# Splitting the expert weights into halves on ScalarE and VectorE instead of GpSimd, with the float32 blocks moved one place and a new order of issue

## The chip, the cores and the metric

One core of one Trainium2 chip. The metric is the device time of one execution in microseconds (us), median of the runs. The work is clustered attention for 4 batches of 768 tokens with 8 heads of 64, followed by a feed-forward layer (512 to 2048 to 512) on the 3072 tokens.

## The reference

```python
def _attn_ref(q, k, v, centroids):
    ...
    q_assign = np.argmax(np.einsum('bhsd,hcd->bhsc', q_n, c_n), axis=-1)
    k_assign = np.argmax(np.einsum('bhsd,hcd->bhsc', k_n, c_n), axis=-1)
    mask = q_assign[:, :, :, None] == k_assign[:, :, None, :]
    scores = scale * np.matmul(q, k.transpose(0, 1, 3, 2))
    scores = np.where(mask, scores, -1000000000.0)
    ...
    return np.matmul(attn, v).astype(np.float32)

def _moe_ref(x, w_in, w_out):
    h = x @ w_in
    ...
    g = np.where(pos, h, np.where(neg, 0.0, (h + beta) ** 2 / (4.0 * beta)))
    return (g @ w_out).astype(np.float32)
```

`q_n`, `k_n`, `c_n` are the rows divided by their norms, `attn` is the softmax over the keys, `pos` and `neg` are `h >= 1` and `h <= -1`. `w_in` and `w_out` arrive as float64.

## The kernel before, in words

**Units.** The tokens of a batch are cut into three chunks of 256 queries; a chunk of a batch is a unit `u`, 12 in all. A unit has four head pairs `hp`, and a pair has four score tiles of 128 queries by 768 keys (`at_scores`): 192 tiles. TensorE writes a tile to PSUM (`pair`), VectorE adds the bias for the cluster mask, takes it to SBUF (`sS`, a ring of three buffers) and finds the row's bound `sbi` in one custom instruction, ScalarE takes the exponential (`at_soft`), casts it to float16 as `hl`'s first half, GpSimd subtracts to get the second half, and a DMA transposes both into `pT`. `at_av` multiplies by the values. For unit 0 transposes by TensorE stand in place of the DMA. From step 22 on the scores use `pair[0]` alone; `pair[1]` gathers the feed-forward layer's output.

**Precision.** Matmuls of float32 accuracy are made from float16 halves: a value is scaled by a power of two, `hi` is its cast, `lo` is the value minus `hi`, and three products of halves are summed. Unit 0 is the exception: its feed-forward layer multiplies in float32, straight from the weights' float32 blocks, since the halves are not there yet.

**Weights.** The feed-forward layer goes by 8 blocks `f` of 256 hidden columns; each has a block of `w_in` (`a = 0`) and one of `w_out` (`a = 1`), 16 blocks `i = 2f + a` of 128 x 1024 values. `w_load` brings one as float64, `w_bits` makes float32 of its bits (a shift and two bit operations on VectorE, an absolute value on ScalarE, sums on TensorE, their maximum `w_am`), `w_bound` makes the scales `w_sw` for four `f` at a time (`GF = 4`), and `w_split` makes the halves `w1[f]`, `w2[f]`.

All 16 blocks lie in one tensor `wb`, 1024 words a block. The float32 values of block `i` lie at place `i` (`w32`, line 1049), and so do the halves: 2 x 1024 float16 values fill the same 1024 words. So `w_split` first copies the scaled values out, to a buffer `tf`, and then writes over the block (line 1138):

```python
tf = wk[1].bitcast(F32) if f < EARLY_SPLITS else new("ws", [1024], F32)
...
rec.scalar.activation(out=tf, in_=w32[a][f].bitcast(F32), func=AF.Copy, scale=w_sw[:, f, a : a + 1])
rec.scalar.copy(whi, tf)
rec.gpsimd.tensor_tensor(out=wlo, in0=tf, in1=whi, op=ALU.subtract)
```

For the first four `f` (`EARLY_SPLITS`) `tf` is `wk[1]`, for the rest a ring of `wk[0]` and the two halves of `word`. These buffers serve other ends too: `wk[0]` is a scratch of `w_bits`, `wk[1]` takes half of the last raw block, `word` is a raw block's place, and all of them are among the seven buffers of the ring `x`, which holds the attention output of a unit for its feed-forward layer.

**What sets the order.** No instruction is issued where it is written. `rec` (class `Recorder`) notes each with its cost and what it depends on; `at(step, fn, ...)` gives each function a step; `issue` (line 328) turns the steps into priorities, runs a list scheduler forward and backward `BASE` times over a model of the engines, adds a number of small pseudo-random shifts to the priorities, one for each number in `NUDGES`, and issues in the order of the last forward pass. So every instruction's line in the profile is 342, and groups are told apart by their tiles. Each engine works its own list in order.

Of the kernel before, what the change touches and what calls it, by code (L numbers as in the profile page):

```python
# [11 lines left out]
F32 = mybir.dt.float32  # L12
U32 = mybir.dt.uint32
AF = mybir.ActivationFunctionType
# [26 lines left out]
TURN, TURN_WAIT = dict(vector=185, gpsimd=118), 200  # L41

LOOK, MARGIN = 0.4, 4000
BASE = 9
NUDGES = (
# [17 lines left out]
)  # L63
TILED = 248

# [400 lines left out]
def tile_clustered_attention_moe(  # L466
# [35 lines left out]
    EARLY = 22  # L502
    VL = 9
    VB = 4
    EARLY_SPLITS = 4
    WA, WR = -4, 2.6

    RAW = [3, 4, 5, 6, 7, 4, 5, 6, 0, 7, 6, 7, 0, 7, 0, None]
# [5 lines left out]
    def tiles(name, n, size):  # L514
        return [const.tile([P, size // 4], U32, name=f"{name}{i}") for i in range(n)]
# [17 lines left out]

    wk = tiles("wk", 2, 4096)
    word = tiles("word", 1, 8192)[0]
    rings["w32"], rings["x"] = Ring(wk[:1] + rings["o"].bufs), Ring(tiles("x", 3, 4096) + wk + [word[:, :1024], word[:, 1024:]])
    rings["g"] = Ring(tiles("g", 2, 2048))

    nb = tiles("n", 1, 2 * 3072)[0]
    nats = [nb[:, :768], nb[:, 768:]] + rings["x"].bufs[1:3]  # L540

    wb = tiles("w", 1, 2 * NF * 4096)[0]
    raws = [wb[:, n * 2048 : (n + 1) * 2048] for n in range(NF)]
# [72 lines left out]
    def v_bound(b, hp):  # L616

        if b == 0:
            st = view(slots[hp][:, 1536:2304], [2 * T * D], F32)
        else:  # L620
            st = view(rings["x"].bufs[2], [2 * T * D], F32) if b == 1 else new("vb", [2 * T * D], F32)
            rec.sync.dma_start(st.rearrange("p (h f) -> p h f", h=2), heads(v, b, hp))
        e = BX.setdefault(b, {})
        if hp == 0:
            e["am"] = new("v_am", [NP], BF16, 2)
        rec.vector.tensor_reduce(
            out=e["am"][:, hp : hp + 1], in_=st, op=ALU.max, axis=AX.X, apply_absolute_value=True
        )
# [417 lines left out]

    W = {}
    WL, WS = {}, {}
    w32 = [[wb[:, (2 * f + a) * 1024 : (2 * f + a + 1) * 1024] for f in range(NF)] for a in range(2)]
    w1 = [view(wb[:, 2 * f * 1024 : (2 * f + 1) * 1024], [2, DM // P, 256], F16) for f in range(NF)]  # L1050
    w2 = [view(wb[:, (2 * f + 1) * 1024 : (2 * f + 2) * 1024], [2, 2, DM], F16) for f in range(NF)]

# [3 lines left out]
    WP = {}  # L1056

    wd = 2 if w_wide else 1
    rings["ws"] = Ring([wk[0], word[:, :1024], word[:, 1024:]])

    def w_load(a, f, part=None):

# [73 lines left out]
        rec.vector.reciprocal(sw, iw)  # L1136

    def w_split(a, f):
        tf = wk[1].bitcast(F32) if f < EARLY_SPLITS else new("ws", [1024], F32)
        w = (w1 if a == 0 else w2)[f]  # L1140
        whi, wlo = (w[:, x].rearrange("p a f -> p (a f)") for x in range(2))
        rec.scalar.activation(out=tf, in_=w32[a][f].bitcast(F32), func=AF.Copy, scale=w_sw[:, f, a : a + 1])
        rec.scalar.copy(whi, tf)
        rec.gpsimd.tensor_tensor(out=wlo, in0=tf, in1=whi, op=ALU.subtract)


    F = {}
# [112 lines left out]
    for b in range(B):  # L1260
# [11 lines left out]
        for c in range(NCH):  # L1272
            u = b * NCH + c
            s0 = first(b, 0, c)
            for x, fn in zip((PRO, -9.1, -8.1, -6.1) if u == 0 else (s0 - 14, s0 - 6.8, s0 - 6.4, s0 - 4.5), (q_load, q_scale, q_split, q_assign)):
                at(x, fn, u)
            for hp in range(0, NP, NP if c else 1):
                at(first(b, hp, c) - (5.5 if u == 0 else 3), q_pairs, u, hp, NP if c else 1)
            for hp in range(NP):
                s0 = first(b, hp, c)  # L1280
                for n in range(SC):
                    at(s0 + n, at_scores, b, hp, c, n // CT, n % CT)
                    at(s0 + n + 1, at_soft, b, hp, c, n // CT, n % CT)
                at(s0 + LA - 0.5, at_av, b, hp, c)

            sf = max(sf, s0 + FA, wat[-1] + 3 if u else 0)
            if u == 1 or u and c == 0:
                at(sf - 1, ffn_scale, range(u, (b + 1) * NCH), range(NF))
            for f in range(NF):
                if u == 0:  # L1290
                    sf = max(sf, wat[2 * f + 1] + 2)
                    FS[u, f] = dict(io=1.0, first=f == 0, last=f == NF - 1)
                    for x in range(2):
                        at(max(sf + 3.5, (wat[-1] if f >= EARLY_SPLITS else wat[2 * GF - 1] if f < GF else wat[-1]) + 1), w_split, x, f)
                    if f == EARLY_SPLITS - 1:
                        free = max(sf + 3.5, wat[2 * GF - 1] + 1) + 0.1
                at(sf, ffn1, u, f)
                at(sf + 3, ffn2, u, f)
                sf += 2
    for i in range(2 * NF):  # L1300
        f, a = divmod(i, 2)
        last = max((k for k in range(i) if RAW[k] == RAW[i]), default=None)
        t0 = max(PRO + 2 + i, -1 if not RAW[i] else PRO) if last is None else wat[last | 1] + 0.1
        for p in (None,) if RAW[i] is not None else (0, 1):
            at(max(t0, free) if p is not None else t0, w_load, a, f, p)
            at(wat[i], w_bits, a, f, p)
        if a and f % GF == GF - 1:
            at(wat[i] + 0.5, w_bound, f // GF)
# [40 lines left out]
```

## Time and profile before

| | |
|---|---|
| median of 3 runs | 852.37 us (851.2 to 853.75) |
| profiled execution, its own time | 852.93 us |
| its span from first to last instruction | 851.1 us |
| PE (TensorE) busy | 810.1 us, 95% |
| DVE (VectorE) busy | 635.3 us, 75% |
| ACT (ScalarE) busy | 656.1 us, 77% |
| POOL (GpSimd) busy | 536.2 us, 63% |
| granted TensorE clock, mean | 0.993 |

The profiled execution lies 0.56 us above the median. The busy shares are means over the whole span; the stages differ, so the text reads them by stretch. PEld is the load of a matmul's weights, which runs beside other matmuls. SP issues the DMAs.

### The profile page before, as it was taken

To read this page: it belongs to the slowest core of one execution; us is meant where nothing else is said; L and a number is where in the kernel's file an instruction comes from. 1 tells how busy PE (TensorE), PEld (TensorE's weight loads), DVE (VectorE), ACT (ScalarE), POOL (GpSimd) and SP (SyncE) were. 2 spreads that over 40 slices of the span, in tenths; PEclk is the share of its full clock that TensorE was granted. 3 is DMA by queue.
4 is the path that set the end of the run, shared out by engine and by line. 5 is a ranking of instruction groups with operands and counts; after the bars stand their busy time and mean duration, and the time that the engine had idled before them with its cause. 6 is when DMAs were issued, how large, how long until landed. Compare 5 with 4: busy or idle time off the path is not lost.

```text
span 851.1 us, 18767 instructions
## 1 busy us (share of the span) xinstructions
PE 810.1 (95%) x7052; PEld 558.9 (66%) x7052; DVE 635.3 (75%) x1400; ACT 656.1 (77%) x1166; POOL 536.2 (63%) x510
## 2 busy tenths in 40 slices
PE   3787998999999999999999999999999999999998
PEld 3455675666775676766776667667766667676664
DVE  6999999879886877678888766678888766544322
ACT  7778989899987788688778788788778688776232
POOL 1112799879986678667666778656677667666122
PEclk9999999999999999999999999999999999999999
DMA  9968898798999879898998988999999887665100
GB/s 311 269 138 246 225 204 213 157 172 194 186 172 159 186 128 205 171 185 169 201 187 165 168 160 177 197 170 199 204 155 161 150 162 126 119 123 111 20 25 25
DMA packets 404763, 142.50 MB, mean 167 GB/s; under 512 B 372800, under 2 KB 396352, under 8 KB 404672
## 3 DMA queue, kind: packets, MB, share of 16 engines
q1 hardware_dynamic: 404672, 141.30, 82.1%
q8 instruction: 55, 0.90, 0.4%
q14 instruction: 36, 0.29, 0.1%
HBM read 40.40 MB, written 6.29 MB: 55 GB/s over the span
## 4 chain that ended last, share of the span: by engine, by line
PE 77%; DVE 12%; DMA 4%; issue 3%; ACT 2%; POOL 1%; SPq 0%; DVEq 0%; POOLq 0%; ACTq 0%
PE pair L342 39%; PE banka L342 10%; PE banki L342 9%; PE bankj L342 9%; PE bankh L342 9%; DVE sS L342 3%; DVE w L342 2%; DMA pT<-hl 1%; DVE bankh L342 1%; DMA q<-qn 1%; DMA kv<-n 1%; ACT sS L342 1%; DVE mx L342 1%; DMA kv<-x 1%; POOL hl L342 1%
## 5 line engine op out<-in xcount | busy, mean ns | idle before, releaser
L342 POOL TENSOR_TENSOR hl<-sS,hl 128x768 f16<-128x768 f32 x176 | 301.2, 1716 | 120.7 <-ACT hl L342 105.5
L342 PE MATMUL pair<-w,g 128*128 128x512 f16 (+1 forms) x1120 | 276.7, 392 | 0.7 <-DVE g L342 0.7
L342 ACT ACTIVATE sS<-sS,sbi 128x768 f32<-128x768 f32 x192 | 179.2, 933 | 73.9 <-DVE sbi L342 70.5
L342 DVE CUSTOM_DVE_ANT_0 sS<-pair,zero,er 128x768 f32<-128x768 f32 x192 | 194.3, 1012 | 53.6 <-PE pair L342 32.9
L342 PEld LDWEIGHTS <-w 128*128 128x128 f16 x2112 | 204.9, 98 | 42.7 <-issue 4.5
L342 PEld LDWEIGHTS <-g 128*128 128x128 f16 x1056 | 101.1, 98 | 107.2 <-issue 2.0
L342 PE MATMUL pair<-kv,q 128*128 128x384 f16 x768 | 158.1, 329 | 11.1 <-ACT pT L342 5.0
L342 ACT CAST hl<-sS 128x768 f16<-128x768 f32 x176 | 144.4, 825 | 9.3 <-DMA pT<-hl 7.9
L342 POOL TENSOR_TENSOR g<-r,g 128x512 f16<-128x512 f32 x80 | 96.4, 1205 | 56.4 <-ACT g L342 50.6
L342 PEld LDWEIGHTS <-q 128*128 128x128 f16 x992 | 78.9, 98 | 66.6 <-issue 22.8
L342 PE MATMUL banka<-pT,kv 128*64 128x256 f16 (+1 forms) x1680 | 105.7, 279 | 0.3 <-DMA pT<-hl 0.3
L342 PEld LDWEIGHTS <-kv 128*64 128x64 f16 (+1 forms) x1824 | 92.3, 108 | 5.0 <-DMA kv<-x 1.7
L342 ACT ACTIVATE r<-r,f_ra,f_rs 128x512 f32<-128x512 f32 x80 | 64.8, 810 | 35.0 <-DVE r L342 34.3
L342 PE MATMUL bankj<-x,w 128*128 128x256 f16 (+1 forms) x424 | 59.1, 292 | 0.6 <-DVE g L342 0.4
L342 ACT CAST g<-r 128x512 f16<-128x512 f32 x80 | 48.8, 611 | 11.8 <-DVE r L342 5.9
L342 POOL TENSOR_TENSOR qn<-qn,phi 128x256 f16<-128x256 f16 x48 | 31.9, 684 | 30.3 <-DVE phi L342 19.9
L342 PE MATMUL bankh<-x,w 128*128 128x256 f16 (+1 forms) x376 | 46.7, 277 | 0.6 <-DVE zs L342 0.5
L342 PE MATMUL banki<-x,w 128*128 128x256 f16 (+1 forms) x288 | 40.3, 291 | 0.9 <-DVE r L342 0.9
L342 PE MATMUL banki<-wk,w 128*128 128x256 f16 x312 | 37.0, 273 | 0.0
L342 ACT ACTIVATION_READ_ACCUMULATOR sS<-sS,sbi 128x1 f32 x192 | 36.1, 188 | 0.0
L342 ACT ACTIVATE q<-q,phi 128x512 f16<-128x512 f16 x48 | 33.0, 711 | 2.8 <-DVE phi L342 0.8
L342 DVE TENSOR_SCALAR r<-banki,f_lo,f_hi 128x512 f32<-128x512 f32 x27 | 21.8, 806 | 16.0 <-PE banki L342 10.0
(262 smaller groups left out, 1099.8 us busy)
## 6 DMA issues: line engine op xcount, KB each, us to landing
w<-in_moe_w_out_dram SPq DMA_DIRECT2D x14, 512.0 KB, 4.8
q<-in_q_dram SPq DMA_DIRECT2D x12, 512.0 KB, 5.4
kv<-in_k_dram SPq DMA_DIRECT2D x16, 384.0 KB, 4.0
kv<-in_v_dram SPq DMA_DIRECT2D x16, 384.0 KB, 4.4
out_dram<-o SPq DMA_DIRECT2D x11, 512.0 KB, 3.6
w<-in_moe_w_in_dram SPq DMA_DIRECT2D x10, 512.0 KB, 6.1
word<-in_moe_w_in_dram SPq DMA_DIRECT2D x6, 512.0 KB, 4.3
o<-in_v_dram SPq DMA_DIRECT2D x8, 384.0 KB, 3.9
```

What stands on the lines that cost most here:

```text
L342: fn(*args, **kw)
```

## The change

`w_split` loses its buffer and its GpSimd instruction. ScalarE writes the scaled cast straight to `whi`; VectorE computes value times scale minus `whi` in one instruction into `wlo` (the helper `split`, which `k_split`, `q_split` and `v_split` use). Both read the float32 block, so it must not lie where its own halves go: block `i` now lies at place `i + 1`, and the last in `xs[2]`, the third `x` buffer, which goes to the end of the ring `x`. The ring `ws`, `EARLY_SPLITS` and `free` go; the splits of a group of four `f` may now come as soon as that group's scales are there. `BASE` is 13, and `NUDGES` is another list.

```diff
-BASE = 9
+BASE = 13
 NUDGES = (
-    2100000010, 2100000020, 2100000029, 2100000041, 2100000053, 2100000117, 2100000135, 2100000137,
...
+    2050000002, 2050000003, 2050000007, 2050000022, 2050000023, 2050000032, 2050000033, 2050000038,
...
-    EARLY_SPLITS = 4
...
-    rings["w32"], rings["x"] = Ring(wk[:1] + rings["o"].bufs), Ring(tiles("x", 3, 4096) + wk + [word[:, :1024], word[:, 1024:]])
+    xs = tiles("x", 3, 4096)
+    rings["w32"], rings["x"] = Ring(wk[:1] + rings["o"].bufs), Ring(xs[:2] + wk + [word[:, :1024], word[:, 1024:], xs[2]])
...
-    w32 = [[wb[:, (2 * f + a) * 1024 : (2 * f + a + 1) * 1024] for f in range(NF)] for a in range(2)]
+    w32 = [wb[:, i * 1024 : (i + 1) * 1024] for i in range(1, 2 * NF)] + [xs[2]]
+    w32 = [w32[a::2] for a in range(2)]
...
-    rings["ws"] = Ring([wk[0], word[:, :1024], word[:, 1024:]])
...
     def w_split(a, f):
-        tf = wk[1].bitcast(F32) if f < EARLY_SPLITS else new("ws", [1024], F32)
+        tf, sw = w32[a][f].bitcast(F32), w_sw[:, f, a : a + 1]
         w = (w1 if a == 0 else w2)[f]
         whi, wlo = (w[:, x].rearrange("p a f -> p (a f)") for x in range(2))
-        rec.scalar.activation(out=tf, in_=w32[a][f].bitcast(F32), func=AF.Copy, scale=w_sw[:, f, a : a + 1])
-        rec.scalar.copy(whi, tf)
-        rec.gpsimd.tensor_tensor(out=wlo, in0=tf, in1=whi, op=ALU.subtract)
+        split(whi, wlo, tf, sw)
...
-                        at(max(sf + 3.5, (wat[-1] if f >= EARLY_SPLITS else wat[2 * GF - 1] if f < GF else wat[-1]) + 1), w_split, x, f)
-                    if f == EARLY_SPLITS - 1:
-                        free = max(sf + 3.5, wat[2 * GF - 1] + 1) + 0.1
+                        at(max(sf + 3.5, wat[2 * GF * (f // GF + 1) - 1] + 1), w_split, x, f)
...
-            at(max(t0, free) if p is not None else t0, w_load, a, f, p)
+            at(t0, w_load, a, f, p)
```

The list itself tells nothing; what it does stands in the order that each engine gets. Three places follow. Names carry the number of their buffer; `ISA sS...<-pair...` is the custom instruction that takes a score tile, `v_am` the bound of a head pair's values, `w_78` the tensor `wb`.

VectorE, up to the first score tile, before:

```order
L342 TENSOR_TENSOR er_139<-bankj,zm_143 128x4
L342 TENSOR_REDUCE v_am_155<-kv_61 128x1
L342 TENSOR_REDUCE w_am<-banki 128x2
L342 SCALAR_TENSOR_TENSOR banki<-ik_130,iq_126 128x1
L342 ISA sS_86,sbi_144<-pair_79,zero,er_139 128x768
```

and now (the reduction of `kv_61` stands further ahead, between the query halves and the first key half):

```order
L342 TENSOR_TENSOR er_139<-bankj,zm_143 128x4
L342 SCALAR_TENSOR_TENSOR banki<-ik_130,iq_126 128x1
L342 TENSOR_REDUCE v_am_155<-kv_62 128x1
L342 TENSOR_SCALAR banki<-banki 128x1
L342 TENSOR_REDUCE v_am_155<-kv_63 128x1
L342 TENSOR_REDUCE v_am_155<-kv_64 128x1
L342 RECIPROCAL phi_142<-banki 128x1
L342 ISA sS_86,sbi_144<-pair_79,zero,er_139 128x768
```

All four reductions of batch 0 now stand ahead of the first score tile, where one did.

GpSimd, in the second unit of batch 0, while the float32 feed-forward layer of unit 0 runs, before:

```order
L342 TENSOR_TENSOR rr_159<-rs_149,rr_159 128x4
L342 TENSOR_TENSOR w_78<-wk_70,w_78 128x1024
L342 TENSOR_TENSOR hl_168<-sS_85,hl_168 128x768
L342 TENSOR_TENSOR hl_167<-sS_87,hl_167 128x768
L342 TENSOR_TENSOR w_78<-wk_70,w_78 128x1024
L342 TENSOR_TENSOR x_73<-rb_160,x_73 128x256
L342 CAST rr_157<-rs_150 128x4
L342 TENSOR_TENSOR w_78<-wk_70,w_78 128x1024
L342 TENSOR_TENSOR hl_167<-sS_86,hl_167 128x768
```

and now:

```order
L342 TENSOR_TENSOR rr_159<-rs_149,rr_159 128x4
L342 TENSOR_TENSOR x_73<-rb_160,x_73 128x256
L342 TENSOR_TENSOR hl_167<-sS_87,hl_167 128x768
L342 CAST rr_157<-rs_150 128x4
L342 TENSOR_TENSOR rr_157<-rs_150,rr_157 128x4
L342 TENSOR_TENSOR hl_168<-sS_85,hl_168 128x768
```

The subtractions of weights are gone from the list; the halves of the scores follow each other.

VectorE, at the 45th and 46th score tile, before:

```order
L342 ISA sS_85,sbi_144<-pair_79,zero,er_139 128x768
L342 ISA sbi_144 128x1
L342 TENSOR_SCALAR has_132<-banki 128x32
L342 RECIPROCAL rs_150<-rs_150 128x4
L342 SCALAR_TENSOR_TENSOR r_205<-bankj,f_gs_200,r_205 128x512
L342 TENSOR_SCALAR banki<-banki 128x1
```

and now:

```order
L342 SCALAR_TENSOR_TENSOR w_78<-w_78,w_sw 128x1024
L342 ISA sS_85,sbi_144<-pair_79,zero,er_139 128x768
L342 ISA sbi_144 128x1
L342 SCALAR_TENSOR_TENSOR n_77<-kv_62,sc_136,n_77 128x12x64
L342 TENSOR_TENSOR rb_160<-banka,rb_160 128x256
L342 SCALAR_TENSOR_TENSOR w_78<-w_78,w_sw 128x1024
L342 ISA sS_86,sbi_145<-pair_79,zero,er_139 128x768
L342 ISA sbi_145 128x1
L342 TENSOR_SCALAR r_205<-bankj,f_lo_180,f_hi_175 128x512
L342 TENSOR_TENSOR bankh<-zs_137,has_132 128x64
L342 SCALAR_TENSOR_TENSOR w_78<-w_78,w_sw 128x1024
```

The new instructions (`w_sw` among what they read) stand about one to a score tile here; there are 16, the first ahead of the 31st tile and the last ahead of the 53rd.

## Rows read from the trace of the kernel before

**Rows 1.** Stretch, then busy us of PE, PEld, DVE, ACT, POOL; clock; DMA.
```profile
20.00:94.00 74.00, 57.39 (x531) 39.52 (x529) 71.09 (x169) 57.86 (x98) 18.10 (x21) 0.95 0.87 219
...
131.00:152.00 21.00, 17.15 (x114) 12.78 (x113) 19.43 (x30) 20.20 (x31) 20.94 (x14) 0.92 0.90 214
...
169.00:240.00 71.00, 70.02 (x612) 47.58 (x611) 61.45 (x143) 68.02 (x120) 62.40 (x51) 1.00 0.97 188
...
300.00:852.00 552.00, 546.50 (x4801) 376.57 (x4797) 372.75 (x816) 401.98 (x733) 347.32 (x332) 1.00 0.79 149
```

**Rows 2.** Timeline of VectorE: start, length, instruction, idle time ahead and its releaser.
```profile
13.86 0.43 DVE L342 TENSOR_REDUCE mx<-bankj 128x16 f32<-128x256 f32 x1 [2.39 <-PE bankj L342]
...
23.71 1.02 DVE L342 CUSTOM_DVE_ANT_0 sS<-pair,zero,er 128x768 f32<-128x768 f32 x1 [0.51 <-PE pair L342]
...
93.79 1.01 DVE L342 CUSTOM_DVE_ANT_0 sS<-pair,zero,er 128x768 f32<-128x768 f32 x1
...
147.78 1.02 DVE L342 CUSTOM_DVE_ANT_0 sS<-pair,zero,er 128x768 f32<-128x768 f32 x1 [1.54 <-POOL hl L342]
```

**Rows 3.** Waits of VectorE, 23 to 94: total us, times, longest.
```profile
DVE sS L342 <- PE pair L342: 1.3, 4, 0.5
DVE mx L342 <- PE bankj L342: 0.9, 1, 0.9
```

**Rows 4.** Timeline of GpSimd in the middle.
```profile
130.16 3.12 POOL L342 TENSOR_TENSOR w<-wk,w 128x1024 f16<-128x1024 f32 x1 [1.68 <-ACT w L342]
...
143.97 2.12 POOL L342 TENSOR_TENSOR w<-wk,w 128x1024 f16<-128x1024 f32 x1
146.05 1.69 POOL L342 TENSOR_TENSOR hl<-sS,hl 128x768 f16<-128x768 f32 x1
```

**Rows 5.** Timeline of TensorE in the middle and at 189.
```profile
134.24 3.62 PE L342 MATMUL bankj<-x,w 128*128 128x256 f32 x16
...
142.36 0.81 PE L342 MATMUL pair<-kv,q 128*128 128x384 f16 x4 [3.40 <-DVE sbi L342]
...
144.47 2.95 PE L342 MATMUL bankj<-x,w 128*128 128x256 f32 x8 [0.45 <-DVE g L342]
...
189.06 2.78 PE L342 MATMUL banki<-x,w 128*128 128x256 f16 x24 [0.89 <-DVE r L342]
```

**Rows 6.** The chain that ended last, in order of time: start, us, what.
```profile
31.26 5.83 DMA kv<-n
...
182.68 1.22 POOL w L342
...
184.77 1.17 POOL g L342
```

**Rows 7.** Groups from 94 to 240, all engines: count, busy, mean ns, idle ahead.
```profile
L342 POOL TENSOR_TENSOR w<-wk,w 128x1024 f16<-128x1024 f32 x11 | 27.2, 2469 | 7.2 <-ACT w L342 7.1
L342 ACT CAST w<-wk 128x1024 f16<-128x1024 f32 x11 | 11.5, 1042 | 0.1
...
L342 POOL TENSOR_TENSOR w<-word,w 128x1024 f16<-128x1024 f32 x5 | 10.7, 2132 | 1.6 <-ACT w L342 1.6
```

**Rows 8.** Groups of VectorE from 24 to 94.
```profile
L342 DVE SCALAR_TENSOR_TENSOR w<-w 128x1024 uint32<-128x1024 uint32 x7 | 8.9, 1277 | 0.0
...
L342 DVE TENSOR_REDUCE v_am<-kv 128x1 bf16<-128x768 f32 x3 | 2.8, 941 | 0.0
...
L342 DVE TENSOR_SCALAR wk<-wk 128x1024 uint32<-128x1024 uint32 x3 | 2.1, 687 | 0.0
```

**Rows 9.** VectorE's instructions on `w`, 90 to 170: ns min/median/max.
```profile
L342 DVE SCALAR_TENSOR_TENSOR w<-w x6: 1214/1222/3169, 92.4 to 156.7; 128x1024 uint32<-128x1024 uint32 x6
...
L342 DVE SCALAR_TENSOR_TENSOR w<-word x3: 1218/1628/1742, 112.6 to 159.6; 128x1024 uint32<-128x1024 uint32 x3
```

**Rows 10.** Groups of VectorE from 169 to 240.
```profile
L342 DVE SCALAR_TENSOR_TENSOR o<-wk,o 128x512 uint32<-128x512 uint32 x1 | 2.0, 1980 | 0.0
...
L342 DVE TENSOR_REDUCE aq<-q 128x4 bf16<-128x1024 f32 x1 | 1.2, 1207 | 0.0
```

More of the change, by code (lines that the diff above doesn't have):

```diff
@@ L535, in tile_clustered_attention_moe @@
     word = tiles("word", 1, 8192)[0]
-    rings["w32"], rings["x"] = Ring(wk[:1] + rings["o"].bufs), Ring(tiles("x", 3, 4096) + wk + [word[:, :1024], word[:, 1024:]])
+    xs = tiles("x", 3, 4096)
+    rings["w32"], rings["x"] = Ring(wk[:1] + rings["o"].bufs), Ring(xs[:2] + wk + [word[:, :1024], word[:, 1024:], xs[2]])
     rings["g"] = Ring(tiles("g", 2, 2048))
     nb = tiles("n", 1, 2 * 3072)[0]
-    nats = [nb[:, :768], nb[:, 768:]] + rings["x"].bufs[1:3]
+    nats = [nb[:, :768], nb[:, 768:]] + xs[1:]
     wb = tiles("w", 1, 2 * NF * 4096)[0]
@@ L620, in v_bound @@
         else:
-            st = view(rings["x"].bufs[2], [2 * T * D], F32) if b == 1 else new("vb", [2 * T * D], F32)
+            st = view(xs[2], [2 * T * D], F32) if b == 1 else new("vb", [2 * T * D], F32)
             rec.sync.dma_start(st.rearrange("p (h f) -> p h f", h=2), heads(v, b, hp))
```

32 rows, old and new, of the table NUDGES are left out of this document.

## The prediction

> **What bounds the kernel now.** I read the table in the section on time and profile first, then the busy times by stretch, then the waits and the timelines of the stretches in which TensorE is not full. TensorE is busy for 95% of the span. The table by stretch [rows 1] shows where the rest lies: of the 552 us after 300 it stands 5.5 us, but 16.6 of the 74 us from 20 to 94 and 3.85 of the 21 us from 131 to 152. The change leaves the matmuls as they are, so it can only move the idle time and the slow-clock time of roughly the first 300 us; from there on the end follows TensorE.
>
> I count by **score passes**, VectorE's 192 instructions that take a score tile out of PSUM; the 1st starts at 23.71 and the 21st at 93.79 us [rows 2], the 37th and the 53rd at 169 and 240, the ends of a stretch of the table. So there are three regimes.
> - **Front, passes 1 to 21.** VectorE is busy 71.09 of 74 us [rows 1] and waits 2.2 us on others [rows 3]. It sets the pace.
> - **Middle, passes 21 to 37.** From 131 to 152 GpSimd is busy 20.94 and ScalarE 20.20 of 21 us, VectorE 19.43 [rows 1]. GpSimd stands in the way: a `w` pass of 2.12 us goes ahead of an `hl` pass of 1.69 us [rows 4], and VectorE's score pass at 147.78 waits 1.54 us for that `hl`, since it needs its buffer [rows 2]. TensorE shows the damage: a hole of 3.40 us, another of 0.45, and the first eight float32 records after the hole take 2.95 us, where sixteen took 3.62 ahead of it [rows 5]. The granted clock of the stretch is 0.92 [rows 1]: part of it at 1.2 GHz, behind idle time. A third hole, 0.89 us at 189 [rows 5], ends a chain of GpSimd passes with a `w` pass in it [rows 6].
> - **Back, passes 37 to 53.** TensorE is busy 70.02 of 71 us. VectorE has 71 - 61.45 = 9.55 us free [rows 1].
>
> **The change, part by part.**
>
> *ScalarE loses 16 casts* of 1.04 us [rows 7], 16.7 us; the scaled cast stays and writes the half itself. ScalarE ends none of the holes above, so this is nothing by itself: the queues of GpSimd and VectorE hide it. If those were gone, 20.20 of 21 us says that ScalarE would be next.
>
> *GpSimd loses 16 passes* of 2.13 to 2.47 us, 27.2 + 10.7 = 37.9 us [rows 7]. Three run in the 131 to 152 stretch, the first at 130.16 and the last at 143.97 [rows 4], about 8 us. Without them the 1.54 us wait goes. TensorE's two holes (3.40 + 0.45), the slow records (2.95 - 3.62/2 = 1.14) and the third hole (0.89) add up to 5.9 us, the upper end of this gain. The lower end is nothing: VectorE is busy 19.43 us there and could end the same holes with its own queue. I take **-5.0**, near the upper end, because the row of the wait names GpSimd and because the order puts only 3 of VectorE's 16 new passes ahead of pass 37.
>
> *VectorE gets 16 passes* of 128x1024 with two operands in SBUF. The nearest rows are the weight passes of the same width and kind: 1.28 us in the front [rows 8], medians of 1.22 to 1.63 and a maximum of 3.17 us from 90 to 170, where GpSimd runs beside them [rows 9]. I take 1.28, 20.5 us in all, since GpSimd has less to do than in the second row. By the order 13 of them come in the back: 13 x 1.28 = 16.6 us. Two long passes leave the back for other places (1.98 and 1.21 us [rows 10]) and, net, some five small ones, about 4 us together. So 12.6 us are added against 9.55 us free, 3 too much. But the row of 1.98 us is 512 wide: at the rate of 1.28 for 1024 it holds 1.3 us of waiting beside GpSimd, and eight of GpSimd's `w` passes leave this stretch. One such wait less brings the 3 down to **+1.5**. The ends: nothing, if VectorE's waits on ScalarE and GpSimd go too; +7.6, if a pass costs the worst median (13 x 1.63 - 4 - 9.55).
>
> A rule against this part: the Trainium skill, page "SBUF — State Buffer", section "Who interferes with whom", says that a VectorE instruction with two SBUF inputs contends with a GpSimd instruction that reads SBUF, and that whoever issues first holds the shared pair for its whole instruction. By that rule the back costs what rival 3 says, by the rows the +1.5; the maximum of 3.17 us [rows 9] agrees that such waits exist.
>
> *The new list fills the front.* By the two orders VectorE does more ahead of the 21st score pass: three weight passes (1.28 each), one shift (0.69) and one bound of `v` (0.94) [rows 8], 5.5 us; a small reduction more and a reciprocal less cancel against the overlap of neighbours. Part of it lies ahead of the very first pass: three more bounds of `v`, 2.8 us. What can swallow it: the 2.2 us of waits [rows 3] and a part of the 2.39 us at 13.86 [rows 2], ahead of which one bound now stands, 0.94. 5.5 - 2.2 - 0.9 = 2.4, called **+2.5**. The ends: +5.5 (nothing swallowed) and 0 (the front is paced by transfers such as the 5.83 us at 31.26 [rows 6] and not by VectorE). VectorE is nearly full there, so I stay off the lower end.
>
> *The blocks' new places.* The float32 values of block i lie where the halves of block i + 1 go. So ScalarE's pass of block i + 1 waits until VectorE's pass of block i has read, and VectorE's own waits for ScalarE's: a chain of 16 x (1.04 + 1.28) = 37 us, plus hops between engines. By the order it runs from pass 31 to pass 53, over 71 us. I count it at nothing; what would be late is TensorE's second unit, which needs the halves.
>
> **Sum.** -5.0 + 1.5 + 2.5 = -1.0 against the profiled execution's own 852.93 us: 851.9. That execution lies 0.56 above the median shown, so the forecast is **851.4 us**, no difference to speak of. (0.3%, about what a measurement of this kernel can tell from no change, is 2.6 us.)
>
> **The rivals.**
> 1. *Front hidden, middle won.* The passes moved ahead of pass 21 fall into slack that VectorE's rows do not show, and the back has room: 852.4 - 5.0 = 847.4. For it: these passes only come earlier, they are not new work, and what is done early need not be done in the middle. Against it: VectorE's 96% in the front.
> 2. *VectorE becomes the bound in the back*, at passes 37 to 53. It decides once the added passes exceed the free 9.55 us by more than the other terms give back, 2.5 us. At the upper end, +7.6, with +2.5 and -5.0, it gives 852.4 + 5.1 = 857.5. For it: ScalarE's 68.02 and GpSimd's 62.40 of 71 us, all four engines nearly full; behind the front the scores use one PSUM tile, so TensorE's next scores wait when a score pass is late. Against it: 37.9 us leave GpSimd.
> 3. *Each new pass waits for a GpSimd pass.* GpSimd is busy 62.40 of 71 us and an `hl` pass takes 1.69 us [rows 4], so a new pass would mostly meet one and wait half of it: 13 x 0.85 = 11 us on top of the 1.5, with the other terms 862.4. For it: the 3.17 us. Against it: the medians of the same rows, 1.22 to 1.63, not 1.28 + 0.85 = 2.13 [rows 9]. (The hold of "SBUF — State Buffer", the Trainium skill, would act this way; the trace agrees with some waits and not with one at every pass.)
> 4. *The chain of 16 goes late.* ScalarE and VectorE serve in order, so each link can lose some 2 us behind other passes: 37 + 32 = 69 of 71 us, and with a little more TensorE waits some 4 us for the last halves: 855.4. For it: ScalarE's 68.02 of 71 us. Against it: ScalarE loses 16 casts, and the first half of the chain is there long before the last.
>
> **How the numbers follow.** The forecast case 0.45 (its own spread is 848 to 855: 0.08 faster, 0.32 within, 0.05 slower); rival 1 0.29 (0.27 faster, 0.02 within); rival 2 0.18 and rival 3 0.04, slower; rival 4 0.04, half within and half slower. Faster 0.35, within 0.3% 0.36, slower 0.29. The range takes in rivals 1 and 2: low 846, the median less the whole 5.9 of the middle and a little; high 858.5, rival 2 with one us more of the front's upper end. Rival 3 and the sum of all worst ends (852.4 + 7.6 + 5.5 = 865.5) stay out.
>
> **What would show it.** GpSimd's busy time falls by about 38 us, ScalarE's by 17, VectorE's rises by 19 to 23. The middle is right if TensorE has no hole over 1 us and a clock of 1.00 between passes 29 and 33. The front is right if the 21st score pass starts at 95 to 97 us; at 94 or ahead it is rival 1, at 99 the upper end. The back is right if passes 37 to 53 take 71 to 73 us; over 76 is rival 2, and new passes of over 2 us on the mean rival 3. The forecast is wrong if the time lies outside 848 to 855, or if TensorE's idle time after 300 us changes by more than 1 us, for which I know no reason.

## The result, and the profile after

The changed kernel takes **857.08 us** (855.28 to 858.01, 7 runs), the kernel before 852.37 (851.2 to 853.75, 7 runs): a ratio of 1.005, 95% interval 1.0038 to 1.0062. It is slower by 0.5%. The time lies in the range (846 to 858.5), but the likeliest case, no difference at 851.4, did not come; the time is close to that of rival 2 (857.5). The profiled execution took 857.74 us, 4.8 more than that of before (852.93).

The view of busy times by stretch, after (columns as in [rows 1]):
```profile
20.00:94.00 74.00, 55.52 (x531) 38.06 (x530) 72.18 (x173) 55.85 (x95) 13.68 (x21) 0.93 0.86 233
...
131.00:152.00 21.00, 20.90 (x137) 14.38 (x136) 19.49 (x32) 18.55 (x32) 15.04 (x11) 1.00 0.82 189
...
169.00:240.00 71.00, 64.59 (x575) 42.90 (x574) 67.70 (x140) 63.11 (x103) 48.89 (x38) 1.00 0.85 167
...
300.00:852.00 552.00, 549.00 (x4839) 378.10 (x4837) 373.11 (x816) 402.80 (x733) 348.37 (x334) 1.00 0.78 147
```
Against [rows 1]: in the middle TensorE gains, 20.90 us of 21 at a clock of 1.00 where it had 17.15 at 0.92. From 169 to 240 it loses, 64.59 where it had 70.02, and VectorE is now the fullest, 67.70 where it had 61.45. GpSimd falls from 62.40 to 48.89 there.

VectorE's score passes 1, 21, 37 and 53 in its timeline, after:
```profile
25.25 1.00 DVE L342 CUSTOM_DVE_ANT_0 sS<-pair,zero,er 128x768 f32<-128x768 f32 x1
...
94.61 1.02 DVE L342 CUSTOM_DVE_ANT_0 sS<-pair,zero,er 128x768 f32<-128x768 f32 x1
...
165.47 1.00 DVE L342 CUSTOM_DVE_ANT_0 sS<-pair,zero,er 128x768 f32<-128x768 f32 x1
...
240.48 1.01 DVE L342 CUSTOM_DVE_ANT_0 sS<-pair,zero,er 128x768 f32<-128x768 f32 x1
```
Passes 37 to 53 take 240.48 - 165.47 = 75.0 us, where they took 71. The 21st starts 0.8 us later than in [rows 2], the 1st 1.5 later.

To find where time is lost in two lists of different order, I lined the traces up by the matmul work that TensorE had issued (the columns of each matmul added up) and read how much later the same amount is reached. This **lag** against the kernel before, in us, at eight places of before's time; the experiments' rows are explained below. At 93, 102 and 149 us, where float32 matmuls stand in another order in the two lists, the figure shifts by up to 0.9 us with how they are weighted; from 192 on it hardly does.

| before at | 93 | 102 | 136 | 149 | 192 | 250 | 425 | end |
|---|---|---|---|---|---|---|---|---|
| after | +1.7 | +0.3 | 0.0 | -5.2 | -5.9 | +2.8 | +2.8 | +4.8 |
| e1_copy | +1.5 | +0.1 | -0.2 | -5.7 | -6.3 | -2.9 | -3.5 | -1.7 |
| e5_none | +1.0 | -0.5 | -0.8 | -6.2 | -6.8 | -3.0 | -3.6 | -2.4 |
| e12_no_split | +2.3 | +0.9 | +0.6 | -4.9 | -5.6 | -2.2 | -2.8 | -1.7 |
| e4_twice | +0.4 | -1.1 | -1.1 | -5.1 | +2.6 | +32.8 | +32.4 | +34.2 |
| e2_pool | +2.0 | +0.6 | +0.2 | -4.1 | -0.8 | +12.4 | +11.5 | +12.6 |
| e9_act_twice | +2.5 | +1.1 | +0.7 | -3.4 | -2.0 | +13.4 | +12.4 | +14.5 |
| e8_tail | +1.9 | +0.4 | +0.1 | -5.1 | -5.8 | +2.0 | +1.5 | +1.1 |
| e10_head | -0.4 | +5.9 | +8.9 | +3.6 | +3.0 | +11.4 | +10.5 | +11.5 |
| e3_before_dve | -0.9 | +3.2 | +8.7 | +7.4 | +6.8 | +12.4 | +12.7 | +12.2 |
| e7_four_dve | -0.6 | -0.6 | -0.6 | -0.4 | -0.4 | -0.3 | -0.3 | -0.3 |
| e11_four_gone | -0.7 | -0.7 | -0.7 | -4.2 | -4.6 | -1.9 | -1.3 | -1.6 |

So the change costs about nothing by 102 us (+0.3), wins 6.2 us in and behind the middle, loses **8.7 us from 192 to 250**, and 2.0 more behind 425. The sum is 0.3 - 6.2 + 8.7 + 2.0 = 4.8.

What TensorE waits for from 169 to 252, after (total us, times, longest):
```profile
PE banki L342 <- DVE n L342: 1.9, 2, 1.5
PE pair L342 <- DVE sbi L342: 1.4, 3, 0.6
PE bankh L342 <- DVE er L342: 1.4, 1, 1.4
PE pair L342 <- DMA q<-qn: 1.3, 1, 1.3
PE bankj L342 <- DVE r L342: 0.8, 2, 0.6
PE banki L342 <- DVE w L342: 0.2, 1, 0.2
```
Five of the six lines name VectorE, 5.7 us of 7.0; the one hole of before in the back was 0.89 [rows 5].

The new passes themselves: VectorE's group from 169 to 240, then three rows of VectorE's and GpSimd's timelines, after:
```profile
L342 DVE SCALAR_TENSOR_TENSOR w<-w,w_sw 128x1024 f16<-128x1024 f32 x12 | 18.6, 1552 | 0.2 <-ACT w L342 0.2
```
```profile
190.78 2.69 DVE L342 SCALAR_TENSOR_TENSOR w<-w,w_sw 128x1024 f16<-128x1024 f32 x1
...
197.09 1.27 DVE L342 SCALAR_TENSOR_TENSOR w<-w,w_sw 128x1024 f16<-128x1024 f32 x1
...
190.74 1.65 POOL L342 TENSOR_TENSOR hl<-sS,hl 128x768 f16<-128x768 f32 x1 [2.08 <-ACT hl L342]
```
With a thirteenth of 1.28 at 236.7 there are 13, 19.9 us. Ten take 1.27 to 1.37 us. The one at 190.78 begins 0.04 us behind the start of a GpSimd pass that ends at 192.39 and takes 1.4 us longer than its neighbours: it is held for most of the 1.6 us that this pass still has. Two more (1.65 and 2.66) begin while a GpSimd pass runs. The hold of the Trainium skill, page "SBUF — State Buffer", section "Who interferes with whom", is thus seen, at 3 passes of 13 and not at each; the trace gives 3.2 us for it.

### The profile page after: what moved, and what is told of

Read it like the earlier page. It is cut to its first block, busy times and chain, and to the rows that moved or that the text cites. A ratio compares the mean times of both kernels' runs of the same rounds, so it can differ in the third digit from the quotient of the medians.

```text
span 855.9 us, 18731 instructions
## 1 busy us (share of the span) xinstructions
PE 809.3 (95%) x7052; PEld 557.3 (65%) x7052; DVE 644.4 (75%) x1416; ACT 645.3 (75%) x1150; POOL 499.8 (58%) x494
## 4 chain that ended last, share of the span: by engine, by line
PE 68%; DVE 18%; ACT 5%; DMA 4%; issue 3%; POOL 1%; SPq 0%; DVEq 0%; ACTq 0%; POOLq 0%
PE pair L342 34%; PE banka L342 10%; PE bankh L342 9%; PE bankj L342 8%; PE banki L342 8%; DVE sS L342 4%; DVE w L342 2%; DVE r L342 2%; ACT sS L342 2%; DVE bankj L342 2%; DMA pT<-hl 1%; DVE qn L342 1%; DMA q<-qn 1%; ACT hl L342 1%; DVE mx L342 1%
## 5 line engine op out<-in xcount | busy, mean ns | idle before, releaser
L342 DVE CUSTOM_DVE_ANT_0 sS<-pair,zero,er 128x768 f32<-128x768 f32 x192 | 194.2, 1012 | 44.7 <-PE pair L342 32.8
L342 PE MATMUL bankj<-x,w 128*128 128x256 f16 (+1 forms) x328 | 46.5, 294 | 0.2 <-DVE r L342 0.2
L342 ACT ACTIVATE q<-q,phi 128x512 f16<-128x512 f16 x48 | 33.4, 716 | 12.0 <-DVE phi L342 10.1
L342 PE MATMUL bankh<-x,w 128*128 128x256 f16 (+1 forms) x328 | 40.9, 278 | 0.4 <-DVE r L342 0.4
L342 PE MATMUL bankj<-wk,w 128*128 128x256 f16 x288 | 34.5, 273 | 0.6 <-DVE r L342 0.6
L342 PE MATMUL banki<-x,w 128*128 128x256 f16 (+1 forms) x240 | 34.4, 295 | 0.2 <-DVE w L342 0.2
L342 DVE TENSOR_SCALAR r<-bankh,f_lo,f_hi 128x512 f32<-128x512 f32 x27 | 21.8, 809 | 16.8 <-PE bankh L342 14.3
```

Source lines behind the costliest of these rows:

```text
L342: fn(*args, **kw)
```

## The experiments

Where an edit exchanges an instruction, the order stays that of its kernel: the instruction is swapped only when the finished list is issued. In the diffs, `swap` is what is issued in place of the last recorded instruction.

**1. The length of VectorE's pass: e1_copy, e5_none, e4_twice**
```
         split(whi, wlo, tf, sw)
+        swap = nc.vector.tensor_copy(wlo, whi)          # e1_copy
+        swap = nothing; TensorE reads whi for wlo       # e5_none
+        swap = the same instruction, two times          # e4_twice
```


> The changed kernel in its own order; VectorE's new pass over a block of weights (128x1024, two operands, 1.55 us on the mean from score pass 37 to 53) is replaced by a 16-bit copy of the high half into the low half, so the low halves of the weights are left out. Theory (VectorE is what TensorE waits for from pass 37 to 53): the copy should take about 0.35 us, so 13 x 1.2 = 15.6 us leave that stretch, the 8.7 us that it lost against the kernel before come back, passes 37 to 53 take 70 to 72 us where they took 75.0, and the time is 847 to 850 us. Rival (the chain of blocks, the place of the blocks or the order of the new list costs the time, not the length of the pass): ScalarE's pass and the order stay, passes 37 to 53 take 74 to 75 us and the time is 855 to 857.5 us.

> The changed kernel in its own order; VectorE's new pass is left out altogether, and TensorE reads the high half in the low half's place (so the low halves are left out). With the full pass (857.1), twice the pass (887.7) and the copy (851.7) this is the fourth point of a line: seconds of VectorE per block 0, 0.45, 1.55 and some 3.5. Theory (VectorE sets the pace from pass 37 to 53, down to the copy): the 13 copies of 0.45 us were 5.9 us, and 3 to 5 us of them show: 847 to 849 us. Rival (with the copy VectorE is no longer what TensorE waits for; ScalarE's casts or the list cost the 2.9 us that the copy kept): 851 to 852.5 us, the same as with the copy.

> The changed kernel in its own order; each of VectorE's 16 new passes is issued twice. Theory (VectorE sets the pace from pass 37 to 53): 13 x 1.3 to 1.55 = 17 to 20 us more in that stretch, nearly all of which shows: 872 to 878 us. Rival (VectorE has room there and the time is lost elsewhere): 857 to 863 us.

Measured: nothing 850.99 us (ratio to before 0.9988, 0.9971 to 1.0004), the copy 851.71 (0.9992, 0.9978 to 1.0007), the pass 857.08, twice the pass 887.72 (1.0408, 1.0391 to 1.0425). VectorE's groups on `w` from 169 to 240, of the copy and of the doubled pass:
```profile
L342 DVE COPY w<-w 128x1024 f16<-128x1024 f16 x13 | 5.9, 455 | 2.0 <-ACT w L342 2.0
```
```profile
L342 DVE SCALAR_TENSOR_TENSOR w<-w,w_sw 128x1024 f16<-128x1024 f32 x18 | 32.7, 1817 | 0.3
```
The first 5.9 us of VectorE cost 0.7 and the next 14 cost 5.4. Doubled, all passes together take 57.1 us where they took 24.3, and 30.6 of these 32.8 us show; a part of them is slow clock (the granted clock from the 37th to the 53rd score pass is 0.90 there). The four traces, between the starts of score passes 37 and 53, in us:

| | no pass | copy | pass | pass twice | before |
|---|---|---|---|---|---|
| the stretch | 70.6 | 70.7 | 75.0 | 101.4 | 71.1 |
| VectorE busy | 56.1 | 60.5 | 71.7 | 97.8 | 61.6 |
| VectorE idle | 14.5 | 10.2 | 3.3 | 3.6 | 9.55 |

The copies go into idle time. Real passes fill it down to 3.3 us, and no further: with twice the passes 3.6 us stay idle and the stretch grows instead (e8_tail, in the same list there, keeps 3.7). So VectorE has room for about what the copies take, and with the passes it sets the pace. That is the mechanism of the theory, but not its times: the copy was expected at 847 to 850, the kernel without the pass came out at the lower edge of its rival (851 to 852.5), and the doubled pass lies beyond the 872 to 878 expected. The copy does not win back all of the 8.7 us. Without any pass the kernel still loses 3.8 us from 192 to 250 (-6.8 to -3.0), and 850.99 is 6.1 below the whole change. About 6 us is what the passes cost (6.1 by the medians, 5.8 by the lag at 250, 5.3 by the two ratios to the kernel before).

**2. The rest of that loss: e12_no_split**
```
         split(whi, wlo, tf, sw)
+        swap = nothing for both instructions; the first block of each
+        matrix keeps its cast, and TensorE reads that block everywhere
```


> The changed kernel in its own order; of the 16 blocks only the first of each matrix keeps its ScalarE cast, all of VectorE's new passes and the other 14 casts are left out, and TensorE reads the high halves of the first block of the same matrix everywhere (so the halves of the other blocks and all low halves are left out). With VectorE's passes alone left out the kernel took 851.0 us and still lost 3 us between 192 and 250 us; ScalarE was busy 19.91 of 20 us from 185 to 205 and 19.50 of 20 from 205 to 225 there. Theory (ScalarE is the second bound of that stretch): the 12 casts of 1.13 us gone give the 3 us back, the lag behind the kernel before stays near -6 us at 250 us, 847 to 848.5 us. Rival (the new list's order alone, such as the transfer of the queries that TensorE waits 1.68 us for): 850 to 851.5 us.

Measured: 851.07 us (0.9989, 0.9971 to 1.0006), the rival. TensorE's timeline, and the busy times by stretch, of this run:
```profile
215.02 0.50 PE L342 MATMUL pair<-kv,q 128*128 128x384 f16 x2 [2.32 <-DMA q<-qn]
```
```profile
185.00:205.00 20.00, 20.00 (x172) 12.90 (x170) 16.34 (x43) 16.95 (x31) 12.25 (x11) 1.00 1.00 212
205.00:225.00 20.00, 17.68 (x166) 12.31 (x164) 12.98 (x35) 14.01 (x25) 12.51 (x15) 1.00 1.10 208
```
VectorE, ScalarE and GpSimd all have room now, and 2.3 of the 3.4 us that are lost from 192 to 250 stand in one hole: TensorE asks for transposed queries that a DMA has not yet landed, in a stretch in which the DMA share (the column behind the clock) is 1.10. The issues of this transfer (`q<-qn`) and of two loads, in this run and then before:
```profile
207.14 0.37 SPq L342 DMA_DIRECT2D kv<-in_k_dram  x1
207.56 0.48 SPq L342 DMA_DIRECT2D q<-in_q_dram  x1
208.13 1.22 SPq L342 DMA_TRANSPOSE q<-qn  x1
```
```profile
213.08 1.19 SPq L342 DMA_TRANSPOSE q<-qn  x1
...
215.92 0.81 SPq L342 DMA_DIRECT2D kv<-in_k_dram  x1
216.79 0.47 SPq L342 DMA_DIRECT2D q<-in_q_dram  x1
```
The transfer is issued 4.95 us earlier than before, in step with TensorE's lead of some 5 us, but takes 6.8 us to land where it took 2.4. The new list issues two loads, of 384 and 512 KB, right ahead of it; the old list issues them behind it. The longer time goes with them in the other runs too: 6.1 us in e5_none (the second load 0.56 us ahead), 4.7 in the changed kernel (1.73 ahead), 3.8 in e1_copy (2.59 ahead). No run exchanges the loads alone. So under this list a part of what the middle wins is lost again, whoever splits the weights. Of the other 1.1 us, 0.7 stand in three short holes, two of them for transfers; the rest is open.

**3. GpSimd in VectorE's place: e2_pool**
```
         split(whi, wlo, tf, sw)
+        swap = nc.gpsimd.tensor_tensor(out=wlo, in0=tf, in1=whi, op=subtract)
```


> The changed kernel in its own order; in the place of each of VectorE's 16 new passes GpSimd subtracts the high half from the unscaled float32 block (its tensor_tensor, 2.1 to 2.5 us), so the scale of the low halves is left out. ScalarE still has one cast per block. Theory (VectorE's load from pass 37 to 53 is the cost): VectorE loses 20 us there, passes 37 to 53 take 71 to 73 us and the time is 849 to 853 us; in the middle only 3 GpSimd passes come, so its hole stays closed. Rival 1 (order or chain of blocks): 855 to 857.5 us. Rival 2 (GpSimd is then what TensorE waits for, since a link of the chain of blocks is about 1 us longer and stands behind other GpSimd passes): 857 us and over, with holes released by GpSimd.

Measured: 865.02 us (1.0134, 1.0113 to 1.0155), rival 2. TensorE's waits of that run from 185 to 252:
```profile
PE bankh L342 <- DVE er L342: 3.1, 1, 3.1
PE bankj L342 <- DVE r L342: 2.6, 3, 1.3
PE pair L342 <- DMA q<-qn: 2.1, 2, 1.5
PE banki L342 <- POOL w L342: 2.1, 1, 2.1
PE pair L342 <- POOL g L342: 1.9, 2, 1.4
```
With 13 of 16 splits between passes 37 and 53, GpSimd does worse there than VectorE (its rows and those of VectorE both end holes). But the middle still wins 4.1 us, so it is not the move to VectorE that closes the hole.

**4. The move alone, in the old list: e3_before_dve and e7_four_dve**
```
-        rec.gpsimd.tensor_tensor(out=wlo, in0=tf, in1=whi, op=ALU.subtract)
+        swap = nc.vector.tensor_tensor(...)      # all 16; e7_four_dve: blocks 4, 5, 6, 9
```


> The kernel before in its own order and layout; its 16 subtractions go to VectorE (tensor_tensor in the same place of the list), nothing else changes. Theory (the move of the passes to VectorE costs, whatever the list and the layout): TensorE's hole of 3.4 us at 142 goes, but VectorE, busy 19.4 of 21 us there and 61.5 of 71 us in the back, becomes late in both: 854 to 859 us. Rival (the new list or the new places cost the time): the move alone gives back the hole and costs nothing, 847 to 852 us.

> The kernel before in its own order; of its 16 GpSimd subtractions the four that begin at 130.16, 135.62, 143.97 and 182.6 us are done by VectorE in their places, the other twelve stay on GpSimd. Theory (GpSimd is in the way there, and VectorE, busy 19.4 of 21 us, gets 4 x 1.25 us more but loses its waits on GpSimd): 848 to 851 us, so faster than both kernels. Rival 1 (VectorE is already full there, every pass shows): 852.4 + 5 = 855 to 858 us. Rival 2 (both cancel): 851.5 to 854 us.

Measured: 865.82 us (1.0154, 1.0134 to 1.0175) with all sixteen, worse than expected; 853.12 (1.0013, 0.9992 to 1.0034) with four, the second rival. With four, TensorE's holes in the middle are 0.93 and 2.82 us where they were 3.40 and 0.45: nothing is won there. The busy times and TensorE's waits of e3_before_dve from 94 to 131:
```profile
94.00:131.00 37.00, 30.11 (x160) 20.45 (x160) 35.21 (x46) 27.71 (x44) 12.47 (x10) 0.91 0.75 183
```
```profile
PE pair L342 <- DVE g L342: 4.4, 2, 3.2
PE bankj L342 <- DVE g L342: 2.1, 1, 2.1
```
VectorE is busy 35.21 of 37 us, and TensorE's lag goes from -0.9 at 93 to +8.7 at 136: in the old list the first splits (from 97.4 us on) fall where VectorE is already late. The new list has none of them there, its first begins at 132.0. That makes the move bearable.

**5. What made the holes in the middle: e6_four_none and e11_four_gone**
```
         rec.scalar.activation(out=tf, ...)
         rec.scalar.copy(whi, tf)
         rec.gpsimd.tensor_tensor(out=wlo, ...)
+        blocks 4, 5, 6, 9: the last left out         # e6_four_none
+        blocks 4, 5, 6, 9: all three left out        # e11_four_gone
```


> The kernel before in its own order; the four GpSimd passes over weight blocks that begin at 130.16, 135.62, 143.97 and 182.6 us are left out, and TensorE reads the high half in the low half's place for these four blocks (their low halves are left out). Theory (in the middle these passes stand ahead of GpSimd's passes that free the score tiles, and TensorE's holes of 3.40, 0.45 and 0.89 us follow from that): with them gone 4 to 6 us go, 846 to 848.5 us. Rival (the holes are VectorE's own queue, and the new list, not GpSimd's relief, closed them): 851 to 852.5 us.

> The kernel before in its own order; for the four blocks whose GpSimd passes were left out in an earlier run (those begin at 130.16, 135.62, 143.97 and 182.6 us) the two ScalarE casts are left out as well, and TensorE reads the halves of the first block of the same matrix in their place. That run won 0.8 us at 149 us, its score-pass halves then waited for ScalarE. Theory (ScalarE is the next in the old list there, so that GpSimd's passes and ScalarE's casts together made the holes): the lag at 149 us is -3 to -5 us, and the time 847 to 848.5 us. Rival (VectorE's own order, a weight pass and a label pass ahead of the score pass, made the hole of 3.40 us): the lag stays at -0.8 to -1.5 us, 849.5 to 851.5 us.

Measured: 850.07 us (0.9975, 0.9955 to 0.9994), between theory and rival, and 848.04 (0.9948, 0.9927 to 0.9970), the theory. The profiled executions of both were the longest of their runs (854.84 of ten, 851.29 of six), so I read their traces in the middle alone; the row of e11_four_gone behind 192 is not that of its median. The lag of e6_four_none at 149 is -0.8.

Ahead of the hole of 3.40 us VectorE was not idle, before:
```profile
138.47 2.62 POOL L342 TENSOR_TENSOR hl<-sS,hl 128x768 f16<-128x768 f32 x1
...
139.51 1.87 DVE L342 TENSOR_TENSOR bankh<-zs,has 128x256 f32<-128x256 f32 x1
141.29 1.01 DVE L342 CUSTOM_DVE_ANT_0 sS<-pair,zero,er 128x768 f32<-128x768 f32 x1
```
The label pass `bankh<-zs,has`, 0.42 to 0.45 us when it is undisturbed, takes 1.87 beside the GpSimd pass that ends at 141.09, and the score pass that TensorE waits for stands behind it. That GpSimd pass in turn stood behind a `w` pass that ends at 138.50. GpSimd, VectorE and TensorE there, e6_four_none:
```profile
137.28 2.31 POOL L342 TENSOR_TENSOR hl<-sS,hl 128x768 f16<-128x768 f32 x1 [4.34 <-ACT hl L342]
...
138.01 1.87 DVE L342 TENSOR_TENSOR bankh<-zs,has 128x256 f32<-128x256 f32 x1
...
140.86 0.81 PE L342 MATMUL pair<-kv,q 128*128 128x384 f16 x4 [1.90 <-DVE sbi L342]
...
142.97 3.63 PE L342 MATMUL bankj<-x,w 128*128 128x256 f32 x8 [0.84 <-DVE g L342]
```
The hole of 3.40 us [rows 5] shrinks to 1.90, but GpSimd now stands idle 4.34 us for ScalarE's half. The label pass is held as before, 1.87 us. And the eight float32 records behind the hole take 3.63 us where they took 2.95: still at 1.2 GHz (the granted clock is 0.50 from 143 to 146 us, and before from 144.5 to 146). With ScalarE's casts gone too, TensorE's rows read:
```profile
139.11 0.81 PE L342 MATMUL pair<-kv,q 128*128 128x384 f16 x4 [0.81 <-DVE sbi L342]
...
141.22 1.99 PE L342 MATMUL bankj<-x,w 128*128 128x256 f32 x8 [0.85 <-DVE g L342]
```
The hole is 0.81, the eight records take 1.99 us, 2.4 GHz, and the lag goes from -0.7 to -4.2. So 3.5 us of the holes were the weights' splits in that place, ScalarE's part and GpSimd's together. The new list has put most of these splits off to the back. It has also moved the label pass to 128.18 us, where it takes 0.43; what that gives alone, no run shows.

**6. ScalarE's lost casts: e9_act_twice**
```
         split(whi, wlo, tf, sw)
+        swap = ScalarE's instruction of it, two times
```


> The changed kernel in its own order; ScalarE's scaled cast of each of the 16 blocks is issued twice, so that ScalarE has as many casts (1.13 us each) as in the kernel before, VectorE keeps its passes. Theory (ScalarE's relief is worth nothing by itself, as the prediction had it): 857 to 859 us, the lag behind the kernel before stays at -5 us in the middle (149 us) and +2.8 at 250 us. Rival (ScalarE is as full as VectorE in both places, busy 63.1 of 71 us in the back, and its lost casts pay for the middle): 13 x 1.13 = 14.7 us more against 7.9 free there, 864 to 872 us, and the middle wins 1 to 3 us less.

Measured: 867.66 us (1.0183, 1.0163 to 1.0203), the rival. The stretch from 169 to 240 of this run:
```profile
169.00:240.00 71.00, 58.95 (x488) 38.10 (x487) 60.66 (x117) 67.55 (x102) 39.34 (x34) 0.98 0.79 160
```
ScalarE is at 67.55 of 71 us, and 10.6 us are lost in all: the middle wins 1.8 less (-3.4 against -5.2 at 149), and from there to 250 the loss is 8.8 more. What ScalarE gives up is needed for VectorE's passes to go as they do. The run does not tell ScalarE's load from the chain of blocks: a second cast also makes each link longer, and VectorE stands 5.3 us for a split's cast where it stood 0.2. And it tells of the new list; what the casts cost in the old one is not measured by it.

**7. The two ends of the new list: e10_head and e8_tail**
```
         self.forward(prio)
+        self.order = (what before had issued by the 21st score pass, in its
+                      order) + (the others, in the new order)          # e10_head
+        self.order = (the new order to the 70th score pass)
+                     + (the others in the order of before)             # e8_tail
```


> The changed kernel; all its instructions that the kernel before has issued up to the 21st score pass come first, in the relative order of the kernel before (three weight instructions that wait for others stay behind), everything else follows in the changed kernel's own order. So the weight passes and bounds that the new list had moved ahead of the 21st score pass come behind it again. Theory (the front is neutral: what is done early there costs up to 5 us by 85 us and is given back by 102 us): the lag behind the kernel before is near 0 throughout the front, the middle still wins about 5 us, 856 to 858 us. Rival 1 (the front costs 2.5 us, as predicted): 854 to 855 us. Rival 2 (the early work pays for the middle): the passes come late behind the 21st, the middle wins 0 to 2.5 us, 859 to 862 us.

> The changed kernel; all instructions from the 70th score pass on (about 305 us, where all weights have been split) are issued in the relative order of the kernel before, those ahead of it in the changed kernel's own. Theory (the last 2 us of the loss, between 425 and 505 us, are the new list's order there, which has nothing to do with the weights): 854.5 to 855.5 us, and the lag behind the kernel before stays at 2.5 to 3 us to the end. Rival (they are a late result of the changed front, such as transfers that start later): 857 us as before.

Measured: 863.42 us (1.0131, 1.0116 to 1.0147) with the old front, beyond its second rival; 853.80 (1.0000, 0.9982 to 1.0018) with the old tail. TensorE's row behind the old front, e10_head:
```profile
98.40 1.01 PE L365 MATMUL bankh<-wk,ones 128*128 128x128 bf16 x8 [4.70 <-DVE wk L365]
```
The weight passes that the new list does early are needed right behind the 21st score pass; put there in a bunch, as this mixed order does, they cost 9 us. So the front's some +6 at its worst (at 55 us) is work that is given back by 102. The middle still wins 5.3 us (+8.9 to +3.6), so the early work does not pay for it.

As to the tail, TensorE's three holes in the new list between 425 and 510, after, and the same stretch with the old tail, e8_tail:
```profile
454.69 0.16 PE L342 MATMUL bankh<-aq,ones 128*128 128x4 bf16 x1 [0.71 <-DVE has L342]
...
461.55 0.48 PE L342 MATMUL pair<-kv,q 128*128 128x384 f16 x2 [0.68 <-DMA kv<-n]
...
504.35 0.81 PE L342 MATMUL pair<-kv,q 128*128 128x384 f16 x4 [0.62 <-DVE sbi L342]
```
```profile
425.00:510.00 85.00, 84.88 (x752) 58.81 (x750) 66.98 (x160) 67.61 (x127) 56.88 (x58) 1.00 0.93 173
```
The holes add up to 2.0 us and are gone with the old tail. The code is the same there, so the list alone makes them. The time falls by 3.3 us, somewhat more than the holes and than the theory said; where the rest comes from is open. With the old tail the changed kernel is level with the kernel before. No version that does all of the work was faster than the kernel before; splits shared between VectorE and GpSimd under a list of their own were not tried.

## Why the prediction was wrong, step by step

- **The step that failed: the back, +1.5.** It measured +8.7. The working had the right resource, VectorE, but two steps of it failed. The first: I set the added work against all of the 9.55 us that VectorE had free. Between score passes 37 and 53 its busy time rises by 10.1 us (61.57 to 71.71), less than the 12.6 that I added; yet only some 6 us of the free time could be used, 3.3 stay idle, and the stretch grows by 3.9 us (71.1 to 75.0). In TensorE's lag this is about 6 us of the 8.7 (e5_none). The price of 1.28 us was too low for one pass (1.53 on the mean, 19.9 us for 13), but the passes add only 15.6 us to VectorE's busy time (56.07 to 71.71), since they overlap with their neighbours and some of the other passes get shorter; so that 19.9 - 4 - 9.55 = 6.3 comes near the measured cost is luck. The wait fewer that I took off last did not come, since the new passes were themselves held for 3.2 us (and 3 less the 1.3 of that wait is 1.7, not 1.5). The second: the other 2.6 us of the 8.7 are no cost of the passes. The lead won in the middle runs into a transfer that lands late (e12_no_split). I counted the middle's gain as kept to the end, and did not look for what stands next when TensorE comes early.
- **The middle, -5.0: right in size, wrong in reason.** It measured -5.2 at 149 and -5.9 at 192. I gave it to GpSimd's passes, by the row of the 1.54 us wait. But that wait, ahead of the score pass at 147.78, lies behind both holes (they end at 142.36 and 144.47) and cannot have made them. Without four of GpSimd's passes the old list wins 0.8 (e6_four_none), and 3.5 when ScalarE's casts go with them (e11_four_gone). The text did say that ScalarE would be next. It did not say what that means for the term.
- **ScalarE's casts, "nothing by itself": wrong for the new kernel.** Put back, they cost 10.6 us.
- **The front, +2.5: wrong, as rival 1 argued.** The mark was the 21st pass at 95 to 97; it starts at 94.61, and the lag is +0.3 by 102.
- **TensorE after 300, no change: wrong.** The lag grows by 2.0 us there, by three holes of the new list's own. A list is planned anew as a whole, so code far from the change is ordered anew too.
- **The chain of blocks, nothing: right as far as it shows.** Of TensorE's waits in the back only 0.2 us name `w`, and VectorE waits 0.2 us for a link. ScalarE stands 4.7 us, in five places, for a VectorE pass of the chain; what that does to TensorE is not separated from VectorE's load.
- **Rival 3** has its mechanism (3 of 13 passes) and not its size: a mean of 1.53 us, under the 2 us that I had set as its mark. **Rival 2** has the time and the place, by a sum whose terms are not quite mine: +8.7 where it had +7.6, a front that costs nothing where it had +2.5, a middle of -6.2 and a tail of +2.0. That it comes within half a microsecond is luck, and its mark, passes 37 to 53 in over 76 us, is not met (75.0).
- **The counts.** GpSimd's busy time falls by 36.4 us (38 said), ScalarE's by 10.8 (17 said), VectorE's rises by 9.1 (19 to 23 said). By groups ScalarE's instructions do lose 16.8 us; busy time counts overlaps once. VectorE's 16 new passes are 24.3 us over the whole span, more than said, but others are shorter in sum, such as the 12 weight passes `w<-w` (17.0 to 14.7; the one of 3.17 us [rows 9] is gone) and the 24 passes `qn<-zs` (10.6 to 7.2). From 169 to 240, where it counts, VectorE is 6.25 us busier (67.70 less 61.45), in a stretch that had 9.55 us free and in which it is now the last that TensorE waits for.

## What to carry to other kernels

When work moves to an engine, compare it with that engine's free time in the very stretch where it lands, and do not count all of that time as usable: 4.4 us of copies into 14.5 free cost 0.7, and 11.2 us more into the 10.2 left cost 5.4 and still left 3.3 idle. In a stretch where three engines are all over 90% busy, a hole can belong to the work that they share: here taking away one engine's part won little (0.8 us) until the other's went too (3.5). Before a wait is called the cause of a hole, see that it lies ahead of it. And a lead won early is only kept if transfers and the other engines come early as well; a new list has to be paid for over the whole kernel, not only around the change.

## What the runs showed of the hardware

A VectorE pass with two operands in SBUF can be held until a GpSimd pass is nearly or wholly done: the 128x256 label pass of 0.43 us took 1.87 us in e6_four_none, and ended 0.29 us behind the GpSimd pass that had begun ahead of it (137.28 + 2.31 = 139.59, 138.01 + 1.87 = 139.88); before, it took the same 1.87 us and ended as far behind (141.38 against 141.09). I had not expected it for a pass that short, and it stood right ahead of the score pass that TensorE waited for. Nearly halving a hole can also leave the slow clock behind it: with the hole at 1.90 us the eight float32 records took 3.63 us, with 3.40 us 2.95, with 0.81 us 1.99, so 1.5 us of hole gave 0.8 of lag.
